# Tile 1 of layer one transposed by a DMA, other dummies at the start, and new engine lists up to K'V

## The chip, the cores and the metric

The kernel runs on one core of one Trainium2 chip. A core has five engines that run their own instruction lists and meet at semaphores: TensorE (PE; its weight loads are shown apart, as PEld), VectorE (DVE), ScalarE (ACT), GpSimd (POOL) and SyncE (SP), which issues DMAs. The metric is the device time of one execution in microseconds (us), as the median of several runs.

## What is computed

Two layers, each a linear attention and an MLP, on x of 2048 tokens by 512, in bfloat16; both layers use the same weights.

```python
def _A_ref(x, wqkv, wo):
    H = 32; Dh = D // H
    q, k, v = qkv[0], qkv[1], qkv[2]
    phi = lambda t: jnp.where(t > 0, t + 1, jnp.exp(t)) + 1e-6
    pq, pk = phi(q), phi(k)
    kv = jnp.einsum("bhsd,bhse->bhde", pk, v)
    z = jnp.einsum("bhsd->bhd", pk)
    num = jnp.einsum("bhqd,bhde->bhqe", pq, kv)
    den = jnp.einsum("bhqd,bhd->bhq", pq, z)[..., None] + 1e-6
    o = num / den
...
    h = _gelu(jnp.einsum("bsd,df->bsf", y, w1) + b1)
    return jnp.einsum("bsf,fd->bsd", h, w2) + b2
...
x = x + _A_ref(_layernorm(x, axis=-1), A_wqkv, A_wo)
x = x + _B_ref(_layernorm(x, axis=-1), B_w1, B_b1, B_w2, B_b2)
x = x + _A_ref(_layernorm(x, axis=-1), A_wqkv, A_wo)
x = x + _B_ref(_layernorm(x, axis=-1), B_w1, B_b1, B_w2, B_b2)
```

## The kernel before

The 2048 tokens are 16 tiles of 128, in four chunks of four tiles. Layer one takes the chunks in the order 3, 0, 1, 2, so tiles 12 to 15 come first, then 0 to 3 and so on. A helper records every operation with what it reads and writes, and a scheduler then issues each engine's operations strictly in the order of a list written out by hand in `CONF["ORDER"]`; waits follow from the recorded reads and writes. An engine whose next operation is not ready stands still, whatever is behind it. The scheduler's own clock decides only which buffer and which PSUM bank an operation gets.

The names in the lists carry the layer, then the tile (or chunk and part). For layer one (0), tile t:

- `statsA0_t`, `aggrA0_t` (DVE), `vepsA0_t`, `powA0_t`, `nmrA0_t` (mostly POOL), `normA0_t` (DVE or ACT): the layer norm of a tile. Tiles 12 to 15 take a variant, in which the mean is subtracted first (`cenA0_t`), and `yscA0_t` scales later; tile 13 has its statistics from ACT (`sumA0_13`, `sqA0_13`).
- The normed tile is turned so that the model dimension lies on the partitions. Either by PE, as four 128x128 transposes into a PSUM bank (`PTA0_t`, L806) and a copy out of it by ACT (`tcA0_t`, L816); or by one DMA transpose on SP's queue (`TA0_t`, L793). The table `CONF["WAY"]` says which.
- `K0_t` (L861): the keys of a tile, four matmuls of 512 columns. `Q0_c_k` (L879 and L892): the queries of chunk c. `expk`, `reluk` (ACT, L831 and L842), `mink`, `phik` (mostly DVE, L844, L848; where `WAY` says "max", L835 and L837): phi of the keys; `expq` to `phiq` the same for queries.
- `G0_t_p` (L962): instead of K'V, the kernel gathers K'y over all tiles in four PSUM banks that are held throughout, and multiplies with the weights of V once at the end (`KV0_p`, L1017). `Z0_c` (L943): the sums of the keys. `D0_c_k` (L1086): denominators, with `ln0`, `rec0` on ACT. `M0_p` (L1040): K'V with `wo` folded in. `WO0_t` (L1110): the output of the attention. `W10`, `W20` (L1142, L1181): the MLP. `RA0_t` adds the residual.
- POOL issues the late loads of the weights (L683): `wv`, `wo`, and `w1` and `w2` in two halves each. All of them, as well as `b2` and `Tb1` (the transpose of the bias b1) on SP, wait until the last DMA transpose of layer one's first norm has landed.

PE starts with dummies on constants (`warm`, `N_WARM` of 512 columns and `N_WARM2` of 128, L699), then transposes tile 12, runs eight more narrow dummies (`idle0_0`), transposes tile 13, and so on. Each of the first tiles goes the way: centred on DVE, transposed on PE, copied by ACT, read by its K.

The PE transpose of tile 1 holds one of the at most two PSUM banks that such transposes may have at a time, and its copy stands in ACT's list between `reluq0_3_3` and `yscA0_15`.

Of the kernel before, what the change touches and what calls it, by code (L numbers as in the profile page):

```python
# [282 lines left out]
def assign_waits(graph, order, sems, dma_sems):  # L283
# [56 lines left out]
    N_WARM2=4, N_IDLE=[8, 1], XQ='sp', WKQ='sp act', WK1=1,  # L340
    LAND={'x0': 3220, 'x1': 4450, 'wk1': 5200, 'wk0': 6080, 'x2': 6750, 'wq': 8250, 'xc0': 9520, 'xc1': 10800, 'xc2': 12050},
    C0=(3, 0, 1, 2), N_WARM=8, ZC=(0, 3), LQ='sp', N_HALF=1, N_K=4, N_Q=3, P_Z0=6.15, N_PB=1, N_PT=8, P_DEN=-50.43,
# [4 lines left out]
            "warm PTA0_12 idle0_0 PTA0_13 K0_12 idle0_1 K0_13 PTA0_14 Q0_3_0 Q0_3_2 PTA0_15 G0_12_0 K0_14 K0_15 "  # L347
            "Q0_3_3 Q0_3_1 G0_13_0 PTA0_1 G0_14_0 K0_0 Z0_3 G0_15_0 K0_1 K0_3 K0_2 Q0_0_2 Q0_0_3 G0_0_0 G0_1_0 Q0_0_0 "
            "K0_8 G0_2_0 G0_3_0 K0_5 Z0_0 K0_4 K0_6 K0_7 Q0_0_1 K0_10 K0_11 Q0_1_0 K0_9 Q0_1_3 Z0_1 G0_4_0 Z0_2 "
            "Q0_1_2 Q0_1_1 G0_5_0 D0_0_3 D0_0_0 G0_6_0 D0_0_1 G0_7_0 D0_0_2 G0_8_0 ZR0 G0_9_0 G0_10_0 G0_11_0 G0_11_2 "  # L350
            "D0_1_0 G0_11_1 Q0_2_0 G0_11_3 KV0_0 D0_1_1 KV0_1 D0_1_2 KV0_2 KV0_3 Q0_2_1 M0_1 M0_2 M0_0 M0_3 Q0_2_2 "
            "WO0_0_0 WO0_0_1 WO0_0_2 WO0_0_3 D0_1_3 WO0_1_0 WO0_3_0 WO0_2_0 Q0_2_3 WO0_5_0 WO0_4_0 WO0_6_0 PTB0_0 "
            "WO0_7_0 W10_0_12_0 W10_0_11_0 W10_0_13_0 W10_0_9_0 W10_0_5_0 W10_0_3_0 W10_0_4_0 W10_0_6_0 W10_0_0_0 "
            "W10_0_1_0 W10_0_8_0 W10_0_7_0 W10_0_10_0 W10_0_13_1 W10_0_4_1 W10_0_7_1 W10_0_0_1 W10_0_2_0 W10_0_11_1 "
            "WO0_8_0 W10_0_3_1 W10_0_12_1 W20_1_0 W10_0_5_1 W10_0_2_1 W20_1_7 W10_0_10_1 W10_0_6_1 W10_0_9_1 W20_0_0 "
# [25 lines left out]
            "reluq0_3_2 expq0_3_0 expk0_14 reluk0_14 normA0_3 expq0_3_2 expk0_15 reluk0_15 reluq0_3_3 tcA0_1 yscA0_15 "  # L381
            "expk0_0 expq0_3_3 reluq0_3_1 expq0_3_1 reluk0_1 expk0_1 normA0_5 normA0_8 expk0_2 reluq0_0_2 normA0_10 "
            "reluk0_3 expq0_0_3 expk0_3 normA0_6 normA0_7 expk0_8 expq0_0_0 expq0_0_2 reluq0_0_0 reluk0_5 expk0_5 "
            "expk0_4 normA0_9 reluk0_6 expk0_6 expk0_7 reluq0_0_1 expq0_0_1 expk0_10 expk0_11 reluk0_11 expk0_9 "
            "reluk0_9 expq0_1_3 expq0_1_2 expq0_1_0 reluq0_1_2 expq0_1_1 ln0_0_0 rec0_0_0 ln0_0_1 rec0_0_1 ln0_0_3 "
            "rec0_0_3 reluq0_1_1 cpz0 ln0_0_2 rec0_0_2 ln0_1_0 expq0_2_0 rec0_1_0 ln0_1_1 b1c rec0_1_1 cpm0_1 cpm0_0 "
            "cpm0_3 ln0_1_2 rec0_1_2 ln0_1_3 rec0_1_3 expq0_2_1 expq0_2_3 reluq0_2_1 reluq0_2_3 expq0_2_2 tcB0_0 "
# [91 lines left out]
            "x0 x1 wk0 x2 wq xc0 xc1 xc2 TA0_0 TA0_3 TA0_2 TA0_5 TA0_8 TA0_4 TA0_6 TA0_7 TA0_10 TA0_11 TA0_9 b1 b2 "  # L479
            "Tb1 TB0_1 TB0_2 TB0_3 TP0_2_0 TB0_5 TB0_7 TB0_6 TB0_4 TP0_3_1 TP0_3_0 TP0_3_3 TP0_2_3 TP0_2_1 TP0_2_2 "  # L480
# [7 lines left out]
        "TA0_0": "dma", "TA0_1": "pe", "TA0_10": "dma", "TA0_11": "dma", "TA0_12": "pe", "TA0_13": "pe", "TA0_14": "pe",  # L488
# [55 lines left out]
def build_kernel(nc, A_x, A_wqkv, A_wo, B_x, B_w1, B_b1, B_w2, B_b2, out, conf=None, report=False):  # L544
# [5 lines left out]
    with ExitStack() as es:  # L550
# [827 lines left out]
```

## Time and profile before

| what | value |
|---|---|
| median of 3 runs | 325.02 us (324.99 to 325.56) |
| the profiled execution's own time | 325.09 us |
| its span in the trace | 323.4 us |
| granted TensorE clock | 1.00 |
| PE busy | 319.9 us, 1725 matmuls |
| DVE, ACT, POOL busy | 215.5, 195.1, 135.4 us |

The times in the trace count from the start of the span. PE's row counts the time in which a matmul is under way; matmuls overlap, so the ends of neighbours lie over each other. A view of waits says who waited for whom; the chain of waits follows back, from the last instruction, what released each step. SPq and POOLq are the DMA queues of SP and POOL: the row of a DMA's issue is not that of its transfer.

### The profile page before, as it was taken

To read this page: it belongs to the slowest core of one execution; us is meant where nothing else is said; L and a number is where in the kernel's file an instruction comes from. 1 tells how busy PE (TensorE), PEld (TensorE's weight loads), DVE (VectorE), ACT (ScalarE), POOL (GpSimd) and SP (SyncE) were. 2 spreads that over 40 slices of the span, in tenths; PEclk is the share of its full clock that TensorE was granted. 3 is DMA by queue.
4 is the path that set the end of the run, shared out by engine and by line. 5 is a ranking of instruction groups with operands and counts; after the bars stand their busy time and mean duration, and the time that the engine had idled before them with its cause. 6 is when DMAs were issued, how large, how long until landed. Compare 5 with 4: busy or idle time off the path is not lost.

```text
span 323.4 us, 4794 instructions
## 1 busy us (share of the span) xinstructions
PE 319.9 (99%) x1725; PEld 159.1 (49%) x1725; DVE 215.5 (67%) x506; ACT 195.1 (60%) x335; POOL 135.4 (42%) x224
## 2 busy tenths in 40 slices
PE   8999999999999999999999999999999999999996
PEld 4444545675444444444444444458644444444443
DVE  5998769999985660214759999999898664000232
ACT  5999698873136129488974657879913734576000
POOL 4672278638703359000366645873902934000000
PEclk9999999999999999999999999999999999999999
DMA  7514458212320105310003200121252243000004
GB/s 246 175 39 94 146 144 305 60 34 59 72 49 12 39 16 99 67 32 2 0 0 68 49 16 2 23 59 36 50 84 49 49 53 79 16 0 2 32 25 155
DMA packets 47572, 20.52 MB, mean 63 GB/s; under 512 B 42620, under 2 KB 46076, under 8 KB 47548
## 3 DMA queue, kind: packets, MB, share of 16 engines
q1 hardware_dynamic: 46076, 15.19, 20.9%
q0 software_dynamic: 1056, 4.72, 4.6%
q10 hardware_dynamic: 416, 0.30, 0.3%
q8 instruction: 14, 0.23, 0.3%
q14 instruction: 10, 0.08, 0.1%
HBM read 8.00 MB, written 2.10 MB: 31 GB/s over the span
## 4 chain that ended last, share of the span: by engine, by line
PE 92%; DVE 6%; POOL 1%; issue 0%
PE ps L1142 30%; PE ps L1181 29%; PE ps L861 9%; PE ps L1110 7%; PE ps L962 4%; PE ps L892 3%; PE ps L879 3%; PE ps L994 2%; PE ps L699 1%; PE ps L1168 1%; DVE gtb L1007 1%; DVE rd L1065 1%; PE ps L943 1%; DVE xsb L1115 1%; DVE gacc L1004 1%; PE ps L1086 1%
## 5 line engine op out<-in xcount | busy, mean ns | idle before, releaser
L1148 ACT ACTIVATE gT<-ps,b1c 128x512 bf16<-128x512 f32 (+1 forms) x140 | 77.2, 600 | 64.4 <-PE ps L1142 63.5
L1142 PE MATMUL ps<-t,w 128*128 128x512 bf16 (+1 forms) x560 | 101.3, 337 | 0.0
L1181 PE MATMUL ps<-w,gT 128*128 128x512 bf16 x434 | 98.4, 379 | 0.0
L1142 PEld LDWEIGHTS ps<-t,w 128*128 128x128 bf16 x560 | 54.5, 98 | 43.8 <-ACT t L816 0.3
L1181 PEld LDWEIGHTS ps<-w,gT 128*128 128x128 bf16 x434 | 42.3, 98 | 50.2
L758 POOL TENSOR_TENSOR rstd<-veps,neghalf 128x1 f32<-128x1 f32 x64 | 39.3, 627 | 5.0 <-DVE veps L756 2.8
L831 ACT ACTIVATE eb<-ps 128x512 bf16<-128x512 f32 x56 | 32.4, 605 | 11.3 <-PE ps L879 3.7
L1191 DVE TENSOR_TENSOR pkb<-ps,xsb 128x512 bf16<-128x512 f32 x15 | 10.2, 685 | 41.5 <-PE ps L1181 41.5
L743 DVE BATCH_NORM_STATS2 stats<-xsb 128x6 f32<-128x512 f32 x48 | 32.1, 677 | 0.3
L861 PE MATMUL ps<-wqkv,t 128*128 128x512 bf16 x128 | 31.4, 379 | 0.0
L1110 PE MATMUL ps<-gtb,t 128*128 128x512 bf16 x128 | 31.3, 380 | 0.1
L842 ACT ACTIVATE rb<-ps 128x512 bf16<-128x512 f32 x38 | 22.8, 607 | 9.3 <-PE ps L861 7.0
L748 POOL TENSOR_SCALAR veps<-mv 128x1 f32<-128x1 f32 x32 | 9.0, 282 | 42.9 <-DVE mv L745 40.9
L756 POOL TENSOR_SCALAR veps<-mv 128x1 f32<-128x1 f32 x28 | 7.1, 258 | 45.5 <-DVE mv L745 44.1
L778 ACT ACTIVATE yb<-xsb,nmr,rstd 128x512 bf16<-128x512 f32 x21 | 16.7, 812 | 11.4 <-POOL nmr L775 11.4
L783 DVE TENSOR_SCALAR yb<-xsb,mv,rstd 128x512 bf16<-128x512 f32 x27 | 14.9, 560 | 11.9 <-POOL rstd L758 11.6
L1187 DVE TENSOR_TENSOR xsb<-ps,xsb 128x512 f32<-128x512 f32 x16 | 10.9, 682 | 16.8 <-PE ps L1181 16.8
L879 PE MATMUL ps<-wqkv,t 128*128 128x512 bf16 x80 | 20.2, 379 | 0.0
L1110 PEld LDWEIGHTS ps<-gtb,t 128*128 128x128 bf16 x128 | 12.3, 98 | 14.8 <-ACT gtb L975 0.3
L861 PEld LDWEIGHTS ps<-wqkv,t 128*128 128x128 bf16 x128 | 12.3, 98 | 14.8 <-ACT t L816 0.3
L844 DVE TENSOR_SCALAR eb<-eb 128x512 bf16<-128x512 bf16 x46 | 13.8, 312 | 8.2 <-ACT eb L831 8.0
L1127 POOL TENSOR_TENSOR xsb<-xsb,b2b 128x512 f32<-128x512 f32 x14 | 17.1, 1218 | 1.0 <-DVE yb L783 0.7
(103 smaller groups left out, 395.0 us busy)
## 6 DMA issues: line engine op xcount, KB each, us to landing
w<-in_B_w_dram POOLq DMA_DIRECT2D x4, 896.0 KB, 7.5
out_dram<-pkb SPq DMA_DIRECT2D x15, 128.0 KB, 2.0
t<-in_A_x_dram SPq DMA_DIRECT2D x3, 512.0 KB, 6.7
t<-yb SPq DMA_TRANSPOSE x57, 2.5
wqkv<-in_A_wqkv_dram SPq DMA_DIRECT2D x1, 512.0 KB, 5.2
wqkv<-in_A_wqkv_dram POOLq DMA_DIRECT2D x1, 512.0 KB, 4.3
wo<-in_A_wo_dram POOLq DMA_DIRECT2D x1, 512.0 KB, 5.7
t<-t SPq DMA_TRANSPOSE x20, 2.5
```

The costliest lines, as they stand in the source:

```text
L743: G.op("dve", lambda e: e.bn_stats(stats[:, s.slot, :], src()), 602, reads=src_keys, writes=[k + "s"], tiles=[s, *src_tiles], prio=prio, n ...
L758: G.op("pool", lambda e: e.tensor_tensor(rstd[:, s.slot:s.slot + 1], veps[:, s.slot:s.slot + 1], neghalf[:], op=ALU.pow), 530, reads=[k + ...
L778: G.op("act", lambda e: e.activation(yb[:, y.slot, :], src(), ACT.Identity, bias=nmr[:, s.slot:s.slot + 1], scale=rstd[:, s.slot:s.slot + 1]),
L831: G.op("act", lambda e: e.activation(eb[:, et.slot, :], bank(bt), ACT.Exp, scale=factor()), 569 if by else 483, reads=[src_key, *more], wr ...
L842: G.op("act", lambda e: e.activation(rb[:, rt.slot, :], bank(bt), ACT.Relu, scale=factor()), 569 if by else 478, reads=[src_key, *more], w ...
L861: ins = e.matmul(bank(b), lhsT=yTa(yT)[:, dt, k * P:(k + 1) * P], rhs=wqkv[:, dt, D:2 * D], start=(dt == 0), stop=(dt == DT - 1))
L879: ins = e.matmul(bank(b), lhsT=yTa(yT)[:, dt, k * P:(k + 1) * P], rhs=wqkv[:, dt, 0:D], start=(dt == 0), stop=(dt == DT - 1))
L1110: ins = e.matmul(bank(wb), lhsT=yTa(pq)[:, kt, k * P:(k + 1) * P], rhs=gtb[:, kt, :], start=(kt == 0), stop=(kt == DT - 1))
L1127: G.op("pool" if on_pool else "dve", lambda e: e.tensor_tensor(xsb[:, st, :], xsb[:, st, :], b2b[:], op=ALU.add), 1120 if on_pool else 600 ...
L1142: ins = e.matmul(bank(b, n), lhsT=w1[:, dt, ft * P:(ft + 1) * P], rhs=yTa(yT)[:, dt, k0 * P:k1 * P], start=(dt == 0), stop=(dt == DT - 1))
L1148: G.op("act", lambda e, ft=ft, b=b, k0=k0, k1=k1, n=n: e.activation(gT[:, g.slot, ft * 512 + k0 * P:ft * 512 + k1 * P], bank(b, n), ACT.Ge ...
L1181: ins = e.matmul(bank(b), lhsT=gT[:, g.slot, ft * 512 + k * P:ft * 512 + (k + 1) * P], rhs=w2[:, ft, :], start=(ft == 0), stop=(ft == FT - 1))
```

## The change

Tile 1 of layer one goes from PE to the DMA transpose: `PTA0_1` and `tcA0_1` are gone from the lists, `TA0_1` comes into SP's. The dummies ahead of the first transpose are seven wide and nine narrow ones instead of eight and four. And the lists of all five engines are written anew for the stretch up to K'V; behind KV0_0 the list of PE is what it was. On POOL `w1_0`, `w1_1`, `wv` and `w2_1` now follow one another directly. No function is changed.

```diff
-    N_WARM2=4, N_IDLE=[8, 1], XQ='sp', WKQ='sp act', WK1=1,
+    N_WARM2=9, N_IDLE=[8, 1], XQ='sp', WKQ='sp act', WK1=1,
...
-    C0=(3, 0, 1, 2), N_WARM=8, ZC=(0, 3), LQ='sp', N_HALF=1, N_K=4, N_Q=3, P_Z0=6.15, N_PB=1, N_PT=8, P_DEN=-50.43,
+    C0=(3, 0, 1, 2), N_WARM=7, ZC=(0, 3), LQ='sp', N_HALF=1, N_K=4, N_Q=3, P_Z0=6.15, N_PB=1, N_PT=8, P_DEN=-50.43,
...
         "pe":
-            "warm PTA0_12 idle0_0 PTA0_13 K0_12 idle0_1 K0_13 PTA0_14 Q0_3_0 Q0_3_2 PTA0_15 G0_12_0 K0_14 K0_15 "
-            "Q0_3_3 Q0_3_1 G0_13_0 PTA0_1 G0_14_0 K0_0 Z0_3 G0_15_0 K0_1 K0_3 K0_2 Q0_0_2 Q0_0_3 G0_0_0 G0_1_0 Q0_0_0 "
-            "K0_8 G0_2_0 G0_3_0 K0_5 Z0_0 K0_4 K0_6 K0_7 Q0_0_1 K0_10 K0_11 Q0_1_0 K0_9 Q0_1_3 Z0_1 G0_4_0 Z0_2 "
-            "Q0_1_2 Q0_1_1 G0_5_0 D0_0_3 D0_0_0 G0_6_0 D0_0_1 G0_7_0 D0_0_2 G0_8_0 ZR0 G0_9_0 G0_10_0 G0_11_0 G0_11_2 "
-            "D0_1_0 G0_11_1 Q0_2_0 G0_11_3 KV0_0 D0_1_1 KV0_1 D0_1_2 KV0_2 KV0_3 Q0_2_1 M0_1 M0_2 M0_0 M0_3 Q0_2_2 "
+            "warm PTA0_12 idle0_0 PTA0_13 K0_12 idle0_1 K0_13 PTA0_14 Q0_3_0 Q0_3_2 PTA0_15 G0_12_0 K0_14 Q0_3_3 "
+            "K0_15 Q0_3_1 G0_13_0 K0_0 G0_14_0 K0_1 G0_15_0 K0_2 G0_0_0 Q0_0_2 K0_3 G0_1_0 Q0_0_3 G0_2_0 K0_5 K0_8 "
+            "Z0_3 G0_3_0 Q0_0_0 K0_4 Q0_0_1 K0_6 K0_11 K0_7 Z0_0 G0_4_0 K0_10 K0_9 Z0_1 Q0_1_2 Q0_1_3 Q0_1_0 Z0_2 "
+            "G0_5_0 Q0_1_1 D0_0_0 G0_6_0 D0_0_1 G0_7_0 D0_0_2 D0_0_3 G0_8_0 D0_1_0 G0_9_0 G0_10_0 G0_11_0 G0_11_1 ZR0 "
+            "G0_11_2 Q0_2_0 G0_11_3 KV0_0 D0_1_1 KV0_1 D0_1_2 KV0_2 KV0_3 Q0_2_1 M0_1 M0_2 M0_0 M0_3 Q0_2_2 WO0_0_0 "
...
         "act":
             "wk1 sumA0_13 tcA0_12 sqA0_13 tcA0_13 expk0_12 reluk0_12 tcA0_14 expk0_13 reluq0_3_0 reluk0_13 tcA0_15 "
-            "reluq0_3_2 expq0_3_0 expk0_14 reluk0_14 normA0_3 expq0_3_2 expk0_15 reluk0_15 reluq0_3_3 tcA0_1 yscA0_15 "
-            "expk0_0 expq0_3_3 reluq0_3_1 expq0_3_1 reluk0_1 expk0_1 normA0_5 normA0_8 expk0_2 reluq0_0_2 normA0_10 "
-            "reluk0_3 expq0_0_3 expk0_3 normA0_6 normA0_7 expk0_8 expq0_0_0 expq0_0_2 reluq0_0_0 reluk0_5 expk0_5 "
-            "expk0_4 normA0_9 reluk0_6 expk0_6 expk0_7 reluq0_0_1 expq0_0_1 expk0_10 expk0_11 reluk0_11 expk0_9 "
-            "reluk0_9 expq0_1_3 expq0_1_2 expq0_1_0 reluq0_1_2 expq0_1_1 ln0_0_0 rec0_0_0 ln0_0_1 rec0_0_1 ln0_0_3 "
-            "rec0_0_3 reluq0_1_1 cpz0 ln0_0_2 rec0_0_2 ln0_1_0 expq0_2_0 rec0_1_0 ln0_1_1 b1c rec0_1_1 cpm0_1 cpm0_0 "
+            "reluq0_3_2 expq0_3_0 reluk0_14 expk0_14 expq0_3_2 expk0_15 yscA0_15 reluk0_15 normA0_3 expq0_3_1 expk0_0 "
+            "reluq0_3_1 normA0_8 reluk0_1 expk0_1 normA0_5 reluq0_3_3 expk0_2 reluq0_0_2 expq0_0_2 normA0_7 expq0_0_3 "
+            "expq0_3_3 expk0_3 reluk0_3 normA0_6 reluk0_5 expk0_5 expk0_8 normA0_10 expq0_0_0 reluq0_0_0 expk0_4 "
+            "normA0_9 expk0_6 reluk0_6 reluq0_0_1 expk0_11 expk0_7 reluk0_11 expq0_0_1 expk0_10 expk0_9 reluk0_9 "
+            "expq0_1_3 expq0_1_2 expq0_1_0 reluq0_1_2 expq0_1_1 ln0_0_0 ln0_0_1 rec0_0_0 reluq0_1_1 rec0_0_1 ln0_0_3 "
+            "rec0_0_3 ln0_0_2 rec0_0_2 cpz0 ln0_1_0 expq0_2_0 rec0_1_0 ln0_1_1 b1c rec0_1_1 cpm0_1 cpm0_0 cpm0_3 "
...
         "dve":
...
-            "mink0_13 statsA0_1 aggrA0_3 normA0_0 phik0_13 statsA0_2 aggrA0_1 aggrA0_2 mink0_14 yscA0_13 statsA0_10 "
-            "normA0_1 yscA0_14 phik0_14 normA0_2 minq0_3_0 mink0_15 statsA0_5 phik0_15 phiq0_3_0 aggrA0_5 aggrA0_10 "
-            "minq0_3_2 statsA0_8 zs0_3 phiq0_3_2 aggrA0_8 mink0_0 statsA0_6 statsA0_4 statsA0_7 aggrA0_4 aggrA0_7 "
-            "aggrA0_6 phik0_0 statsA0_9 mink0_1 minq0_3_3 aggrA0_9 mink0_2 phik0_1 phik0_2 minq0_3_1 normA0_4 "
-            "statsA0_11 minq0_0_3 mink0_3 phiq0_3_3 phiq0_0_3 phik0_3 aggrA0_11 phiq0_3_1 mink0_8 phik0_8 minq0_0_0 "
+            "mink0_13 statsA0_1 aggrA0_3 aggrA0_1 normA0_0 statsA0_2 phik0_13 aggrA0_2 normA0_1 yscA0_13 mink0_14 "
+            "phik0_14 normA0_2 yscA0_14 statsA0_8 mink0_15 aggrA0_8 phik0_15 statsA0_7 statsA0_5 minq0_3_1 mink0_0 "
+            "minq0_3_0 aggrA0_5 phik0_0 statsA0_11 phiq0_3_1 statsA0_6 aggrA0_7 mink0_1 phiq0_3_0 phik0_1 minq0_3_2 "
+            "aggrA0_11 aggrA0_6 statsA0_4 mink0_2 aggrA0_4 phik0_2 phiq0_3_2 statsA0_9 statsA0_10 normA0_4 aggrA0_10 "
+            "mink0_3 minq0_0_3 phik0_3 aggrA0_9 phiq0_0_3 normA0_11 minq0_3_3 minq0_0_2 zs0_3 mink0_5 mink0_8 "
...
         "pool":
             "id0 bdm0 neghalf id1 bdm1 powA0_12 vepsA0_13 eps6 powA0_13 powA0_14 vepsA0_0 powA0_15 b1z powA0_0 "
-            "vepsA0_3 powA0_3 nmrA0_3 vepsA0_1 powA0_1 vepsA0_2 powA0_2 vepsA0_5 powA0_5 nmrA0_5 vepsA0_8 powA0_8 "
-            "vepsA0_10 powA0_10 nmrA0_10 nmrA0_8 vepsA0_7 vepsA0_4 powA0_7 powA0_4 vepsA0_9 vepsA0_6 powA0_6 powA0_9 "
-            "nmrA0_7 nmrA0_6 vepsA0_11 powA0_11 nmrA0_9 phik0_6 w1_1 phiq0_1_2 wv wo w2_1 phiq0_1_1 w1_0 pr0_0_2 "
+            "vepsA0_1 powA0_1 vepsA0_2 powA0_2 vepsA0_3 powA0_3 nmrA0_3 vepsA0_8 powA0_8 nmrA0_8 vepsA0_5 powA0_5 "
+            "nmrA0_5 vepsA0_7 vepsA0_6 powA0_7 nmrA0_7 vepsA0_4 powA0_4 vepsA0_11 powA0_6 nmrA0_6 vepsA0_10 powA0_11 "
+            "powA0_10 vepsA0_9 powA0_9 nmrA0_9 nmrA0_10 phik0_6 w1_0 w1_1 wv w2_1 phiq0_1_2 phiq0_1_1 wo pr0_0_2 "
...
         "sp":
-            "x0 x1 wk0 x2 wq xc0 xc1 xc2 TA0_0 TA0_3 TA0_2 TA0_5 TA0_8 TA0_4 TA0_6 TA0_7 TA0_10 TA0_11 TA0_9 b1 b2 "
-            "Tb1 TB0_1 TB0_2 TB0_3 TP0_2_0 TB0_5 TB0_7 TB0_6 TB0_4 TP0_3_1 TP0_3_0 TP0_3_3 TP0_2_3 TP0_2_1 TP0_2_2 "
+            "x0 x1 wk0 x2 wq xc0 xc1 xc2 TA0_0 TA0_1 TA0_2 TA0_3 TA0_8 TA0_5 TA0_7 TA0_4 TA0_6 TA0_11 TA0_10 TA0_9 b1 "
+            "Tb1 b2 TB0_1 TB0_2 TB0_3 TP0_2_0 TB0_5 TB0_7 TB0_6 TB0_4 TP0_3_1 TP0_3_0 TP0_3_3 TP0_2_3 TP0_2_1 TP0_2_2 "
...
     WAY={
-        "TA0_0": "dma", "TA0_1": "pe", "TA0_10": "dma", "TA0_11": "dma", "TA0_12": "pe", "TA0_13": "pe", "TA0_14": "pe",
+        "TA0_0": "dma", "TA0_1": "dma", "TA0_10": "dma", "TA0_11": "dma", "TA0_12": "pe", "TA0_13": "pe", "TA0_14": "pe",
```

## The prediction, made before the result was known

> **What bounds the kernel now.** I read the page first: the span and the engines.
>
> ```profile
> span 323.4 us, 4794 instructions
> PE 319.9 (99%) x1725; PEld 159.1 (49%) x1725; DVE 215.5 (67%) x506; ACT 195.1 (60%) x335; POOL 135.4 (42%) x224
> ```
>
> TensorE is busy in 319.9 of 323.4 us, but a busy PE row may hide short waits, because ends of matmuls are modelled. So the view of waits comes next, for PE alone, and it has a single line, the start of the kernel:
>
> ```profile
> PE ps L699 <- PEq L1363: 0.8, 1, 0.8
> ```
>
> Next the busy time by stretch (columns: window, its length, then PE, PEld, DVE, ACT, POOL with counts, clock, share of DMA, GB/s), for the stretch that the change reorders:
>
> ```profile
> 10.00:22.00 12.00, 12.00 (x77) 5.83 (x76) 11.96 (x40) 12.00 (x22) 8.28 (x23) 1.00 0.25 66
> 22.00:34.00 12.00, 12.00 (x71) 5.63 (x70) 9.40 (x31) 11.51 (x22) 4.38 (x12) 1.00 0.43 88
> 46.00:58.00 12.00, 12.00 (x69) 5.88 (x68) 10.90 (x23) 10.05 (x20) 9.59 (x12) 1.00 0.88 290
> ```
>
> PE is full in all of it; from 10 to 22 us DVE (11.96 of 12) and ACT (12.00 of 12) are full as well. The chain of waits gives the same picture step by step (start, length, what):
>
> ```profile
> 0.83 4.00 PE ps L699 x12
> 4.83 0.43 PE ps L806 x4
> 5.26 0.72 PE ps L699 x8
> 5.98 0.22 PE ps L806 x4
> 6.20 0.86 PE ps L861 x4
> ...
> 15.52 0.22 PE ps L806 x4
> ...
> 51.07 0.86 PE ps L1040 x4
> ```
>
> The first five groups begin each where the last ends, and so it goes on through the stretch. Four 128-wide transposes take 0.43 us at 4.83 and 0.22 us at 5.98: the array runs at half speed until about 5.7 us, and at full speed after. The reader is to see that the end of this kernel is the sum of what PE issues: the change can move it only by what it takes from or adds to PE's list, or by a wait that PE does not have today.
>
> **The change, part by part.**
>
> *The transpose taken off PE.* PTA0_1 is the group of four at 15.52: it goes, minus 0.22 us. Nothing hides behind it, since PE is gapless there, so the whole of it counts. Its copy out of PSUM, tcA0_1, goes from ACT as well (first row below): 0.69 us of relief for an ACT that is full, worth nothing to the end directly, because PE is no faster for it, but slack for the new lists.
>
> ```profile
> 16.37 0.69 ACT L816 ACTIVATE t<-ps 128x512 bf16<-128x512 bf16 x1
> 12.15 1.30 SPq L793 DMA_TRANSPOSE t<-yb  x1
> SPq L793 <- ACT eb L831: 11.9, 5, 6.0
> t<-yb SPq DMA_TRANSPOSE x57, 2.5
> ```
>
> *The transpose put on SP's queue.* One more DMA transpose: 1.30 us of issue, 2.5 us to landing. The queue of SP waits 11.9 us in five waits before such transposes (third row, the queue's own waits; the longest 6.0), so there is room for 1.3 us more. Who needs it, and when? In the new list K0_0 stands directly behind G0_13_0, where the transpose stands today: at 15.52, or 15.63 with the dummies' 0.11 (below). Then G0_14_0 and K0_1, 0.86 us each step (a group of four, as in the row at 6.20): K0_1 at 17.35. TA0_0 starts at 12.15 as today and lands at 12.15 + 2.5 = 14.65, one us ahead of K0_0. TA0_1 needs normA0_1, today the DVE step at 14.24:
>
> ```profile
> 14.24 0.41 DVE L783 TENSOR_SCALAR yb<-t,mv,rstd 128x512 bf16<-128x512 bf16 x1
> ```
>
> In the new list a min, a scaling and a statistic no longer stand ahead of it, so it can be done behind TA0_0's issue, at 13.5, and TA0_1 lands at 16.0. Even where it is today, done at 14.65, the transposed tile is there at 17.15, still before 17.35. So both cost nothing; without that cover the price is the lateness itself, one for one, paid by K0_1 and all behind it. The transposes behind, up to TA0_9, are shifted into the queue's waits.
>
> *The dummies.* One wide less, five narrow more. The weight loads show the half-speed steps: 0.15 busy after 0.28 idle, so 0.43 us, for a wide one, and 0.86 us for eight narrow, 0.107 each.
>
> ```profile
> 3.34 0.15 PEld L699 LDWEIGHTS ps<-const-bfloat16-1.0 128*128 128x128 bf16 x1 [0.28 <-issue]
> 4.94 0.86 PEld L699 LDWEIGHTS ps<-const-bfloat16-1.0 128*128 128x128 bf16 x8
> 5.29 0.60 ACT L816 ACTIVATE t<-ps 128x512 bf16<-128x512 bf16 x1 [0.49 <-PE ps L806]
> 5.79 0.71 ACT L738 ACTIVATE eb<-t,stats 128x512 bf16<-128x512 bf16 x1
> 6.49 0.59 ACT L816 ACTIVATE t<-ps 128x512 bf16<-128x512 bf16 x1
> 7.13 0.55 PEld L861 LDWEIGHTS ps<-wqkv,t 128*128 128x128 bf16 x4 [0.34 <-ACT t L816]
> ```
>
> Five times 0.107 less 0.43 is +0.11 us before the first transpose. Does it reach the end? The last row says K0_13's weight load waited for ACT. That ACT chain has no air: tcA0_12 starts at 5.29, where the first transposes end (4.83 + 0.43), then sqA0_13, then tcA0_13, back to back, to 7.08. All of it starts 0.11 later, so K0_13 does, and from there PE is full. Bounds: 0 if ACT could catch up, 0.11 if not; the rows show no gap, so I take +0.11.
>
> *K, Q, G, Z and D reordered on PE, with evictions, norms and adds on ACT, DVE and POOL.* The work is the same, so PE's sum is unchanged; the question is only whether some operand is late. The largest jump forward is G0_0_0: two steps (G0_15_0, K0_2) behind K0_1's end, so at about 19.9. It needs phik0_0, which DVE ends at 21.48 today:
>
> ```profile
> 17.51 0.64 ACT L831 ACTIVATE eb<-ps 128x512 bf16<-128x512 f32 x1
> 18.76 1.87 DVE L743 BATCH_NORM_STATS2 stats<-t 128x6 f32<-128x512 bf16 x3
> 20.82 0.66 DVE L837 SCALAR_TENSOR_TENSOR pkb<-ps,eb 128x512 bf16<-128x512 f32 x1
> 23.73 0.68 ACT L842 ACTIVATE rb<-ps 128x512 bf16<-128x512 f32 x1
> ```
>
> Three statistics (1.87 us by the second row), four aggregates, one min and two adds that stand ahead of it today come behind it, one min comes ahead: over 2 us of room. What sets it then is its exponent expk0_0 (first row: 17.51 to 18.15), which the new ACT list does not put later; with a min between, phik0_0 ends by about 19.1, and G0_0_0 has 0.8 us. The other way goes reluk0_3 (last row): two exponents of Q, one of K and normA0_7 come ahead of it, some 0.6 to 0.8 us each, while tcA0_1 and normA0_10 no longer do, so it is about 1.2 us later, 24.9 to 25.6, and G0_3_0 keeps its time on PE: the tightest place I find. I take 0 for the reordering, as every row of PE's list is covered so far as I can follow it, and 0.3 us as the upper bound of the forecast's own case.
>
> *POOL's weight loads.* Now w1_0, w1_1, wv and w2_1 go out one behind the other, and wo comes behind them and behind phiq0_1_1.
>
> ```profile
> 35.20 0.94 POOL L683 DMA_DIRECT2D w<-in_B_w_dram  x1
> 42.98 0.79 POOL L683 DMA_DIRECT2D wqkv<-in_A_wqkv_dram  x1
> 47.52 0.74 POOL L683 DMA_DIRECT2D w<-in_B_w_dram  x1
> w<-in_B_w_dram POOLq DMA_DIRECT2D x4, 896.0 KB, 7.5
> wqkv<-in_A_wqkv_dram POOLq DMA_DIRECT2D x1, 512.0 KB, 4.3
> wo<-in_A_wo_dram POOLq DMA_DIRECT2D x1, 512.0 KB, 5.7
> 43.97 0.63 ACT L1090 ACTIVATE lr<-lr 128x512 f32<-128x512 f32 x1
> 45.74 0.58 ACT L842 ACTIVATE rb<-ps 128x512 bf16<-128x512 f32 x1
> 46.40 1.17 POOL L848 TENSOR_TENSOR t<-eb,rb 128x512 bf16<-128x512 bf16 x1 [0.88 <-ACT rb L842]
> ```
>
> The group at 51.07 above is M0, which reads wo. When does wo land? phiq0_1_1 waits for reluq0_1_1 on ACT, which moves ahead of three logarithm and exponent steps, from 45.74 to 43.97; so phiq0_1_1 goes from 46.40 to about 44.6, ends at 45.8, and wo is issued there. If it lands 4.3 us later, as wv does with nothing queued ahead, that is 50.1; with 5.7, as wo does behind wv, 51.5. M0 needs it at 51.07 - 0.11 = 50.96. Is the queue clear by then? Today wv, wo, w2_1 and w1_0 (2.88 MB) went from 42.98 to about 55.0 (47.52 + 7.5): 0.24 MB/us with the gaps, and 0.29 by the window from 46 to 58. The new queue up to wo's end holds 3.81 MB, from 35.20 on (w1_0 now stands where w1_1 stood): 13.1 to 15.9 us, so 48.3 to 51.1. I take 50.1, with nothing in front, since the four ahead have ten us of their own before it: no wait. Upper bound 51.5: 0.5 us. wv itself is safe: 2.36 MB end by 45.0 at the slower rate, and its first reader comes near 48.9. Tb1 and b2 swap on SP; b2 is read first in the MLP, and the copy of the turned bias stands in ACT's list where it stood: nothing.
>
> *Sum.* Profile's own time 325.09 (span 323.4, and 1.7 around it), minus 0.22, plus 0.11, plus 0: 324.98. The median of the runs is 0.07 below that execution, so 324.91. The forecast's own range runs from no charge for the dummies (324.8) to the reordering's 0.3 on top (325.2). What this kernel's measurement can tell from no change is about 0.2%, 0.65 us; the sum is a sixth of that.
>
> **The rivals.**
>
> *wo late.* M0's four matmuls take over as a wait, since wo now stands behind 3.3 MB. For it: from 46 to 58 the share of DMA is 0.88 today. Against: the queue should be clear. Price 0.5 - 0.11: 325.4; it passes 0.65 us only if wo lands after 51.7.
>
> *Slower: ACT becomes the bound between 22 and 28 us.* Place: reluk0_3 and phik0_3, then G0_3_0, and through the held PSUM banks the next K. It decides once ACT runs about 0.7 us behind the list, which is full (12.00 of 12, then 11.51 of 12), so it cannot recover before 34. Price: two steps, 0.68 + 0.6, about 1.3: 326.2. Against it: ACT has lost 0.69 us of work and DVE none gained.
>
> *The clock rises later.* Half speed ends near 5.7 us, 4.9 after the first dummy. If the new mix of dummies made it rise as late again, at 10.6, PE would do 4.4 us of real work at half speed, about 2.2 us lost: 327.0. Against: PE is as continuously busy as before, and no row ties the rise to width. The Trainium skill (TensorE: Matmul & The Clock Gate, Part 1) says the gate is opened by a free-running window of about 3.4 us of activity, and that the instant differs by about half a us between runs; by that, a window missed would be an estimated 1.7 us and 326.6, and a shift of the instant would touch both kernels alike. The trace agrees with a rise after more than one such window, and shows one execution only.
>
> *Faster by more.* It would need 0.65 us; PE has the 0.22, and a gap before K0_13 that is under 0.34 by the weight load's row. With both and no charge for the dummies 324.5. That the transposition buys nothing at all, because the dummies give 0.11 of it back, is the forecast itself.
>
> **How the numbers follow.** Forecast 0.65; wo late 0.15, of which a third beyond 0.65 us; ACT the bound 0.12, nearly all beyond; the clock 0.03; faster by a gap closed 0.05, mostly still within 0.2%. Slower by over 0.2%: 0.05 + 0.11 + 0.03 = 0.19; faster 0.03; the same 0.78. Predicted 324.9. The range reaches down to 324.5 and up to 326.0, to hold wo late and part of the ACT case.
>
> **What would show it.** Right: sixteen transposes (four tiles) on PE in the first 20 us instead of twenty; K0_13 about 0.11 later; no new line in PE's waits; DMA transposes twelve in the first 33 us; M0 at about 50.9. Wrong: PE idle before L1040 with wo as releaser (first rival), or PE idle between 22 and 34 us behind ACT or DVE; the second four transposes at 0.43 us instead of 0.22 mean the clock. A time over 325.7 or under 324.4 refutes the sum.

## The result, and the profile after

The changed kernel takes 326.22 us (median of 10 runs, 325.44 to 326.83) against 325.24 us of the kernel before on the same chip (10 runs): ratio 1.0024, interval 1.0014 to 1.0034. It is slower by 0.24%, about 0.8 us by the ratio and 1.0 by the medians; the forecast was 324.9, and 326.22 lies over the range's upper end of 326.0. The profiled execution took 326.21 us. Its page begins:

```profile
span 324.5 us, 4796 instructions
PE 319.8 (99%) x1725; PEld 158.7 (49%) x1725; DVE 216.9 (67%) x506; ACT 194.7 (60%) x334; POOL 137.5 (42%) x224
```

PE is busy for as long as before (319.8 to 319.9), so the 1.1 us that the span grew are not work but waits. The view of PE's waits, which had one line, has three:

```profile
PE ps L699 <- PEq L1363: 0.8, 1, 0.8
PE ps L892 <- DMA t<-yb: 0.8, 1, 0.8
PE ps L861 <- DVE pkb L837: 0.3, 1, 0.3
```

L892 waits for a DMA transpose, L861 for DVE. The chain of waits of this kernel (start, length, what) shows where both are:

```profile
17.00 4.35 DMA t<-yb
21.34 0.05 issue
21.39 1.04 PE ps L892 x4
22.43 0.86 PE ps L861 x4
...
30.83 0.18 ACT eb L831
31.01 0.30 issue
31.31 0.58 ACT rb L842
31.90 0.50 ACT eb L831
32.39 0.02 issue
32.42 0.30 DVE eb L835
32.72 0.02 issue
32.74 0.70 DVE pkb L837
33.45 0.04 issue
33.49 1.04 PE ps L861 x4
```

The first is Q0_0_2, the first reader of tile 3's turned tile: TA0_3 went out at 17.00 and landed 4.35 us later, not 2.5. Without a wait Q0_0_2 would have begun at 20.40 (its predecessor's start, 19.54, and 0.86); it began at 21.39: a gap of 0.99. The second is K0_7, which waits for a PSUM bank that phik0_4 (DVE, L837) frees: 33.49 instead of 33.02, 0.47. Note that a wait costs more than the waits view says. In PE's timeline a matmul of 512 columns starts 0.22 us after the one before and its modelled end lies 0.38 after its start, and idle time counts from that end: the 0.83 and 0.30 of idle, each with 0.16 more, are the 0.99 and 0.47. (In the chain such a group stands with 1.04 instead of 0.86.)

The account closes. K0_13 begins at 6.91 instead of 7.13 (below), the transpose saves its 0.22, and two gaps cost 1.46: 1.46 - 0.22 - 0.22 = 1.02 of the 1.1 us of span. All of it lies ahead of M0, which begins at 52.02 instead of 50.91; from there to the end both kernels take 272.45 us (272.44 to 272.55 in all 14 profiles of this document), so nothing behind M0 has a part in it. Busy time by stretch (window, length, PE, PEld, DVE, ACT, POOL with counts, clock, DMA share, GB/s):

```profile
10.00:22.00 12.00, 11.17 (x55) 4.81 (x52) 11.47 (x39) 11.42 (x20) 8.43 (x18) 1.00 0.36 87
22.00:34.00 12.00, 11.70 (x69) 5.37 (x68) 9.53 (x30) 10.26 (x20) 6.30 (x16) 1.00 0.33 66
```

The 0.83 and 0.30 that PE lacks in these two rows are the two waits. ACT is less full than before in both of these stretches (11.42 and 10.26 instead of 12.00 and 11.51), DVE in the first (11.47 instead of 11.96; in the second 9.53 instead of 9.40). Neither is full; each waits in its turn.

Two views show what stood beside the two late operands. In the view of DMA queues for 18.8 to 20.4 us (packets, MB, share of 16 engines) two fetches of instructions, of 16 and 8 KB, lie inside TA0_3's flight:

```profile
q8 instruction: 1, 0.02, 5.5%
...
q14 instruction: 1, 0.01, 1.2%
```

And POOL's small steps are longer. First the kernel after (veps, L756; the power to rstd, L758; nmr, L775), then DVE beside them, then POOL in the kernel before:

```profile
13.32 0.71 POOL L756 TENSOR_SCALAR veps<-mv 128x1 f32<-128x1 f32 x1 [0.38 <-DVE mv L745]
14.11 0.77 POOL L758 TENSOR_TENSOR rstd<-veps,neghalf 128x1 f32<-128x1 f32 x1
...
28.22 0.94 POOL L758 TENSOR_TENSOR rstd<-veps,neghalf 128x1 f32<-128x1 f32 x1
29.26 0.81 POOL L775 TENSOR_SCALAR nmr<-mv,rstd 128x1 f32<-128x1 f32 x2
```

```profile
13.14 0.38 DVE L783 TENSOR_SCALAR yb<-t,mv,rstd 128x512 bf16<-128x512 bf16 x1
13.44 0.35 DVE L768 TENSOR_SCALAR yb<-yb,rstd 128x512 bf16<-128x512 bf16 x1
13.70 0.28 DVE L844 TENSOR_SCALAR eb<-eb 128x512 bf16<-128x512 bf16 x1
14.02 0.42 DVE L848 TENSOR_TENSOR pkb<-eb,rb 128x512 bf16<-128x512 bf16 x1
```

```profile
14.18 0.22 POOL L756 TENSOR_SCALAR veps<-mv 128x1 f32<-128x1 f32 x1
14.48 0.59 POOL L758 TENSOR_TENSOR rstd<-veps,neghalf 128x1 f32<-128x1 f32 x1
```

vepsA0_2 takes 0.71 instead of 0.22, and powA0_2 0.77 instead of 0.59, beside an unbroken row of short bf16 steps on DVE; later powA0_9 takes 0.94, and nmrA0_9 and nmrA0_10 behind it 0.81 together. By the Trainium skill (SBUF — State Buffer, "SBUF: two separate sides"), DVE and GpSimd share a pair of SBUF ports as an exclusive lock, held for the whole instruction by a DVE step in a 2-port mode, or by one with two SBUF inputs against a GpSimd step that reads SBUF, and the loser stands still. These rows agree with it, though they show neither the mode nor the lock.

### The profile page after: what moved, and what is told of

It reads as the page before. It is cut to its first block, busy times and chain, and to the rows that moved or that the text cites. A ratio compares the mean times of both kernels' runs of the same rounds, so it can differ in the third digit from the quotient of the medians.

```text
span 324.5 us, 4796 instructions
## 1 busy us (share of the span) xinstructions
PE 319.8 (99%) x1725; PEld 158.7 (49%) x1725; DVE 216.9 (67%) x506; ACT 194.7 (60%) x334; POOL 137.5 (42%) x224
## 4 chain that ended last, share of the span: by engine, by line
PE 85%; DVE 8%; DMA 3%; POOL 1%; SPq 1%; issue 1%; ACT 0%; ACTq 0%
PE ps L1142 30%; PE ps L1181 29%; PE ps L1110 7%; PE ps L861 6%; PE ps L892 3%; PE ps L962 3%; PE ps L994 2%; PE ps L879 2%; DMA t<-in_A_x_dram 2%; DVE stats L743 1%; DMA t<-yb 1%; PE ps L1168 1%; DVE gtb L1007 1%; DVE rd L1065 1%; POOL rstd L758 1%; PE ps L943 1%
## 5 line engine op out<-in xcount | busy, mean ns | idle before, releaser
L758 POOL TENSOR_TENSOR rstd<-veps,neghalf 128x1 f32<-128x1 f32 x64 | 39.7, 631 | 5.1 <-DVE veps L756 3.0
L831 ACT ACTIVATE eb<-ps 128x512 bf16<-128x512 f32 x56 | 32.3, 600 | 11.8 <-PE ps L879 3.7
L861 PE MATMUL ps<-wqkv,t 128*128 128x512 bf16 x128 | 31.9, 379 | 0.4 <-DVE pkb L837 0.3
L756 POOL TENSOR_SCALAR veps<-mv 128x1 f32<-128x1 f32 x28 | 8.4, 304 | 45.0 <-DVE mv L745 43.6
L748 POOL TENSOR_SCALAR veps<-mv 128x1 f32<-128x1 f32 x32 | 9.1, 284 | 42.8 <-DVE mv L745 40.8
L778 ACT ACTIVATE yb<-xsb,nmr,rstd 128x512 bf16<-128x512 f32 x21 | 16.7, 812 | 11.4 <-POOL nmr L775 11.4
L879 PE MATMUL ps<-wqkv,t 128*128 128x512 bf16 x80 | 20.4, 379 | 0.0
L861 PEld LDWEIGHTS ps<-wqkv,t 128*128 128x128 bf16 x128 | 12.1, 98 | 16.0 <-DVE pkb L837 0.8
```

Of the source, the lines that this page charges most:

```text
L758: G.op("pool", lambda e: e.tensor_tensor(rstd[:, s.slot:s.slot + 1], veps[:, s.slot:s.slot + 1], neghalf[:], op=ALU.pow), 530, reads=[k + ...
L778: G.op("act", lambda e: e.activation(yb[:, y.slot, :], src(), ACT.Identity, bias=nmr[:, s.slot:s.slot + 1], scale=rstd[:, s.slot:s.slot + 1]),
L831: G.op("act", lambda e: e.activation(eb[:, et.slot, :], bank(bt), ACT.Exp, scale=factor()), 569 if by else 483, reads=[src_key, *more], wr ...
L861: ins = e.matmul(bank(b), lhsT=yTa(yT)[:, dt, k * P:(k + 1) * P], rhs=wqkv[:, dt, D:2 * D], start=(dt == 0), stop=(dt == DT - 1))
L879: ins = e.matmul(bank(b), lhsT=yTa(yT)[:, dt, k * P:(k + 1) * P], rhs=wqkv[:, dt, 0:D], start=(dt == 0), stop=(dt == DT - 1))
```

## The experiments

Theory A1: tile 3 now stands fourth on SP's queue, its transpose has 1 us to spare where it had 2.7, and a fetch inside its flight (theory F) uses that up. Theory A2: K0_7's wait comes through POOL and ACT, from the stretched powA0_9 (theory P: POOL's steps are longer beside certain rows of DVE steps) and from nmrA0_10 standing behind it. All runs, each against the kernel before on the same chip:

| kernel | us | before | ratio (95%) |
|---|---|---|---|
| dummies_only | 325.47 | 325.32 | 1.0002 (0.9993 to 1.0011) |
| after_old_dummies | 326.29 | 325.32 | 1.0025 (1.0014 to 1.0037) |
| lists_only | 326.15 | 325.32 | 1.0026 (1.0016 to 1.0036) |
| fetch_later | 326.60 | 325.32 | 1.0037 (1.0025 to 1.0049) |
| nmr10_first | 326.15 | 325.57 | 1.0014 (1.0002 to 1.0026) |
| tile3_early | 325.94 | 325.57 | 1.0013 (1.0004 to 1.0022) |
| both_early | 325.54 | 325.57 | 1.0004 (0.9993 to 1.0015) |
| before_6_13 | 325.55 | 325.57 | 0.9998 (0.9989 to 1.0007) |
| after_again | 326.42 | 325.48 | 1.0037 (1.0022 to 1.0051) |
| dve_order | 326.05 | 325.48 | 1.0021 (1.0013 to 1.0030) |
| dve_order_nmr10 | 325.64 | 325.48 | 1.0005 (0.9997 to 1.0014) |
| tile1_only | 325.79 | 325.48 | 1.0021 (1.0005 to 1.0037) |

**The change taken apart.** dummies_only puts the new dummies into the kernel before; after_old_dummies puts the old ones into the kernel after.

```diff
-    N_WARM2=4, ...  N_WARM=8
+    N_WARM2=9, ...  N_WARM=7
```

> The kernel before with seven wide and nine narrow dummies, nothing else changed. Theory A (a transposed tile, tile 3's, comes late because an instruction fetch of 16 KB runs on the DMA engines while it is in flight: 4.35 us to landing instead of 2.4 to 2.5): the eight added PE instructions bring the fetch from 19.8 to about 19.0 us, where no transpose of this kernel is in flight (one lands at 18.0, the next is issued at 21.6), so nothing comes late; K0_13 starts up to 0.11 later: 325.2 to 325.4. Rival B (the dummies or the clock cost the time by themselves): 326.2.

> The kernel after with eight wide and four narrow dummies as before. Theory A: eight PE instructions fewer ahead of it, the fetch comes about 0.8 us later, at 19.6 to 19.7, when tile 3's transposed tile (issued at 17.0) has all but landed: 2.4 to 2.5 us to landing, no wait of Q0_0_2 (0.99 gone), the second wait of 0.47 behind it smaller or gone: 324.6 to 325.1. Rival B (dummies or clock): the same time, but then the kernel before with the new dummies is slow too. Rival C (tile 3's late place in the lists, without the fetch): 4.3 us to landing again and 326.1. Rival D (the longer SP queue by the tile's move): 326.1 as well.

The dummies cost nothing that can be seen, in either kernel: rival B falls. (325.47 lies just over the 325.2 to 325.4 that were expected; beside the kernel before's 325.32 the ratio is 1.0002.) The second forecast failed: 326.29 instead of 324.6 to 325.1. In its profile the fetch still met TA0_3, only later (at 19.33; landing 3.26 us after issue, 20.32, in time for Q0_0_2), so in this one execution there was no first gap, but K0_7's gap of 0.47 was there all the same. So the second wait does not follow from the first. A new one of 0.31 stood at Q0_0_3, which waited for ACT (eb, L831). This execution had a span of 323.9 us, and its 326.29 lies 2.4 above it; in the other six runs the time is 1.7 to 1.8 above spans of 323.8 to 325.2. So this profile does not show what held the longer of them.

lists_only keeps tile 1 on PE within the new lists:

```diff
-... G0_13_0 K0_0 G0_14_0 ...        (PE)
+... G0_13_0 K0_0 PTA0_1 G0_14_0 ...
-... reluk0_15 normA0_3 expq0_3_1 ... (ACT)
+... reluk0_15 normA0_3 tcA0_1 expq0_3_1 ...
-        "TA0_1": "dma"
+        "TA0_1": "pe"
```

> The new lists alone: eight wide and four narrow dummies, tile 1 turned by TensorE (its four matmuls behind K0_0, the copy behind normA0_3 on ACT, no DMA transpose of it). By 17 us PE has run as many instructions as in the kernel after (eight fewer dummy ones, eight more of the transposes). Theory A: the fetch comes at 18.9 again, tile 3's transpose is in flight from 17.0, lands 1 to 2 us late, Q0_0_2 waits up to 1 us: 325.8 to 326.5. Rival D (the tile's move to the DMA queue costs the time): no late landing, 325.2 to 325.4. Rival C (the lists without the fetch): 326.2.

As A1 said: 326.15, and TA0_3 takes 4.11 us to landing. The gaps in its profile are 0.18 at Q0_0_2, 0.46 at K0_7, and 0.31 at K0_1, which waits for the copy of tile 1 and is this kernel's own. So the late landing and both waits are there without the DMA transpose of tile 1, and rival D is not needed for them. That the time comes out as high as the kernel after's rests in part on the 0.31 that only this kernel has: the two waits are 0.64 here.

tile1_only is the other half, the transpose in the old lists:

```diff
-... G0_13_0 PTA0_1 G0_14_0 ...   (PE)
+... G0_13_0 G0_14_0 ...
-x0 ... TA0_0 TA0_3 TA0_2 ...     (SP)
+x0 ... TA0_0 TA0_1 TA0_3 TA0_2 ...
+            hold = [Tile(psum, "hold", "t0")] if tag == "A0_1" else []
```

> Tile 1 turned by the DMA alone: the kernel before with its lists and dummies, without PTA0_1 and tcA0_1, its DMA transpose second in SP's queue (a PSUM bank stays taken by it, so that the banks of all later steps are as before). Tile 3's transpose now stands third, issued at about 16.2 instead of 14.3, with its first reader K0_3 at 19.4. Theory A1 (it is the place of tile 3 behind tile 1 that is exposed): landing at 18.7 without a fetch, at 20 to 20.5 with one in it; Z0_3 may wait 0.3 for the held bank; 325.3 without the fetch, 325.8 to 326.4 with it. Rival L (the move costs nothing, only the new lists do): 325.1 to 325.4.

Between the two: 325.79, 1.0021, with an interval down to 1.0005; three of its twelve runs took 327.06 to 327.80, and no profile shows why. Its profile has Z0_3's 0.30 for the held bank, an artefact of the experiment, and TA0_3 at 16.38 with 3.55 us to landing, in time for K0_3 at 20.50. Alone, the transposition also moves tile 3 back by 2.1 us, but what it costs without the held bank stays open.

**Where the fetch falls.** fetch_later and before_6_13 were to move the fetch by the number of PE instructions ahead of it.

```diff
-... idle(f"idle{n}_{k}", [P] * cf["N_IDLE"][k], ...      N_IDLE=[8, 1]   (fetch_later)
+... idle(f"idle{n}_{k}", ([P] if k else [D]) * ...       N_IDLE=[2, 1]
-    N_WARM2=4, ... N_WARM=8                               (before_6_13)
+    N_WARM2=13, ... N_WARM=6
```

> The kernel after, with only the filler dummies behind the first transposes changed: two of 512 columns in place of eight of 128, the same columns, twelve PE instructions fewer. Theory A: the fetch comes about 1.2 us later, at about 20.1, behind tile 3's landing; it may hit tile 8's transpose instead (issued at 19.3, its reader is at 25), which has time: no wait of Q0_0_2, 324.8 to 325.3. Rivals B, C and D: nothing that they name has changed, 326.2.

> The kernel before with six wide and thirteen narrow dummies. Theory F (the fetch of instructions delays a transpose in flight): eight more PE instructions than in the run with seven and nine, whose fetch came at 18.16, 0.01 us ahead of tile 2's landing: the fetch now comes at 16.5 to 17.5, inside tile 2's transpose (15.7 to 18.2), which lands 3 to 4.4 us after its issue instead of 2.41; K0_2 needs it at 20.3, so the time stays at 325.3 to 325.6. Rival (the late landings of tile 3 have to do with the new lists or with the transposes around it, not with a fetch): 2.4 to 2.5 us wherever the fetch lies.

In both the 16 KB fetch did not move as expected: it came at 19.04 and at 19.96, in the first inside TA0_3's flight again (4.27 us to landing, a gap of 0.91, and 326.60 instead of 324.8 to 325.3), in the second in no transpose's (the time, 325.55, was as expected under either view, so it decides nothing). What sets its instant stays open. In all 14 profiles the first fetch of this stretch, of 8 or of 16 KB, begins between 17.80 and 19.33: the kernel before has no transpose in flight from 18.01 to 21.58, the kernel after has TA0_3 in flight from 17.00. And after_again, the unchanged kernel after, moved it by itself:

> The kernel after, unchanged, for a second profile and for a comparison on the same chip. Theories A1 and A2: K0_7's gap of 0.47 is there to 0.01 us again, since POOL's powA0_9 takes 0.94 again; Q0_0_2's gap is anything from 0 to 1.0, by whether a fetch falls into tile 3's transpose: 326.0 to 326.5.

In its profile the fetch came at 17.82, inside tile 2's transpose. The chain there:

```profile
16.00 3.97 DMA t<-yb
19.97 0.14 issue
20.11 0.59 PE ps L861 x2
```

Now TA0_2 takes 3.97 us and K0_2 (L861) has the gap, 0.75, while Q0_0_2 has none; K0_7's is 0.47 again. (At the start this execution also waited 0.9 us for a load of weights and 0.3 for tile 12's input.) Same kernel, same lists: what is late is the transpose that meets the fetch. Over all 14 profiles (counted from the records of the DMA queues) layer one has 164 transposes of this kind. 137 landed within 2.56 us of their issue; 27 took 2.66 to 4.35. In 26 of these 27 an instruction fetch was running later than 1.1 us after the issue, and the last stood behind a late one; of the 137 that holds for four, and there the fetch began within 0.25 us of the landing. The 1.1 us were found from these rows; they are not a rule. Later in the kernel, with other transfers about, the tie is looser: of 644 such transposes 94 took over 2.6 us, 86 of these with such a fetch, and 36 with one did not. So fetch and late landing are tied by their instants; that the fetch is the cause was not tested, as no run could place a fetch at will. In the kernel before it was there too, at 31.74 to 34.81, on a tile that PE did not wait for (DMA view of that window):

```profile
q14 instruction: 1, 0.01, 0.6%
...
t<-yb SPq DMA_TRANSPOSE x1, 3.1
```

The Trainium skill (Runtime: NRT & Kernel Launch, "Instruction fetch mechanics") says that an engine refills its instructions in blocks of 16 KiB through a DMA queue of its own, at a cost mostly hidden. The 16 KB packets agree, the 8 KB ones are not in it; here the cost does not stay hidden, if it falls on a neighbour's transfer as these rows suggest.

**The two waits taken away.** nmr10_first moves one step of POOL:

```diff
-... powA0_10 vepsA0_9 powA0_9 nmrA0_9 nmrA0_10 ...
+... powA0_10 nmrA0_10 vepsA0_9 powA0_9 nmrA0_9 ...
```

> The kernel after with one POOL step moved: nmrA0_10 right behind powA0_10, no longer behind nmrA0_9. Theory A2 (K0_7's wait comes through POOL and ACT: powA0_9 takes 0.94 us instead of 0.55, nmrA0_10 stands behind it though its own operand is ready at 26.9, and normA0_10 at the head of ACT's list holds three steps behind it): normA0_10 starts about 0.7 earlier, K0_7's gap of 0.47 is gone, Q0_0_2's wait is as in the kernel after: 326.2 - 0.47, so 325.6 to 325.9. Rival (the second wait is an echo of the first, or phik0_4 is late by something else): the gap stays, 326.2.

The gap at K0_7 is gone. POOL and ACT (normA0_10, L778, which ACT had waited for until 30.11 in the kernel after) and PE's waits in this kernel:

```profile
27.59 0.27 POOL L775 TENSOR_SCALAR nmr<-mv,rstd 128x1 f32<-128x1 f32 x1
28.31 0.22 POOL L756 TENSOR_SCALAR veps<-mv 128x1 f32<-128x1 f32 x1 [0.46 <-DVE mv L745]
28.62 0.95 POOL L758 TENSOR_TENSOR rstd<-veps,neghalf 128x1 f32<-128x1 f32 x1
...
29.61 0.86 ACT L778 ACTIVATE yb<-t,nmr,rstd 128x512 bf16<-128x512 bf16 x1
```

```profile
PE ps L699 <- PEq L1363: 0.8, 1, 0.8
PE ps L892 <- DMA t<-yb: 0.7, 1, 0.7
PE ps L806 <- DVE yb L724: 0.7, 1, 0.7
```

powA0_9 still takes 0.95, but nothing that matters stands behind it. The third line is tile 13's centred input, late at the start of this execution. The time, 326.15, missed the expected 325.6 to 325.9, but the kernel before took 325.57 on this chip. The ratio falls from 1.0024 and 1.0037 to 1.0014, with intervals that overlap: here the trace, and not the time, shows that the wait is gone.

tile3_early removes the first wait, by giving TA0_3 data that is there early:

```diff
-                return e.dma_start_transpose(dst, yb[:, y.slot, :])
+                return e.dma_start_transpose(dst, yb[:, src.slot, :])
+            src, ykey = from0 or (y, ykey)
-... TA0_0 TA0_1 TA0_2 TA0_3 ...
+... TA0_0 TA0_1 TA0_3 TA0_2 ...
```

> The kernel after with tile 3's DMA transpose reading tile 0's normalized tile, which is there at 12.2 us, and issued ahead of tile 2's: it leaves out the use of tile 3's own data in K and Q, all else runs as in the kernel after. Theory A1 (tile 3's turned tile is what Q0_0_2 waits for, in most executions and by up to 0.99): it lands at about 17.3, tile 2's at about 18.6 just ahead of K0_2 at 18.7; no gap at Q0_0_2; the gap of 0.47 at K0_7 stays: 325.4 to 325.8, and the runs lie closer together than the 1.4 us between the kernel after's. Rival (the first wait is a chance of the one profiled execution): 326.2.

> Both edits, nmrA0_10 right behind powA0_10 and tile 3's transpose from tile 0's data: leaves out the use of tile 3's own data in K and Q. Theories A1 and A2 together: no gap on PE but the short one at K0_13; what is left is the sum of the prediction, 324.9 to 325.3. If something else of the change costs time as well, a rest over 325.5 shows it.

tile3_early has no gap at Q0_0_2 and K0_7's 0.47 unchanged (third line of its waits; the first is tile 12's input, late in this execution):

```profile
PE ps L807 <- DVE veps L756: 1.0, 1, 1.0
PE ps L699 <- PEq L1366: 0.8, 1, 0.8
PE ps L862 <- DVE pkb L838: 0.3, 1, 0.3
```

Its ratio is 1.0013 (325.94, over the expected 325.4 to 325.8), and its runs lie within 0.85 us of each other (the kernel after's within 1.4). With both edits the view of PE's waits is:

```profile
PE ps L699 <- PEq L1366: 0.8, 1, 0.8
PE ps L807 <- DVE yb L724: 0.2, 1, 0.2
```

and the kernel takes as long as the one before (1.0004). By the times alone, up to 0.15% could be left, the upper end of the interval; and the expected 324.9 to 325.3 was missed with 325.54: the kernel before took 325.57 on this chip, and the 0.22 of the transpose does not show.

The starts on PE close the account. From tile 14's transposes (PTA0_14) to M0 it takes 42.90 us in the kernel before, so 42.68 without the transpose of tile 1. The kernel after takes 44.23, that is 42.68, the two gaps of 0.99 and 0.47, and 0.09. nmr10_first takes 43.55, which is 42.68 and its one gap of 0.87; tile3_early 43.15, which is 42.68 and 0.47; both edits 43.02. The last 0.34 are two delays too short for the view of waits: 0.17 at K0_2 (19.32), whose transpose this edit puts behind tile 3's (it lands at 19.18), and 0.16 at Q0_0_3, again behind ACT's exponent (L832), as in after_old_dummies. So the two waits are what the change lost, and with them gone two short ones used up the transpose's 0.22 in this profile.

**Two repairs that use all data.** dve_order changes seven steps on DVE, so that a statistic runs beside vepsA0_2; dve_order_nmr10 has nmr10_first's edit as well.

```diff
-aggrA0_2 normA0_1 yscA0_13 mink0_14 phik0_14 normA0_2 yscA0_14 statsA0_8
+aggrA0_2 normA0_1 yscA0_13 statsA0_8 normA0_2 mink0_14 phik0_14 yscA0_14
```

> The kernel after with the order of seven DVE steps changed: statsA0_8 and normA0_2 come ahead of mink0_14 and phik0_14. Theory P (POOL's vepsA0_2 takes 0.71 us instead of 0.22 and powA0_2 0.77 instead of 0.58 because DVE runs a row of short bf16 steps beside them): with a statistic beside them they take about 0.3 and 0.58, so tile 3's normalization and its transpose come about 0.5 earlier (issued at 16.4 to 16.5 instead of 17.0) and Q0_0_2's gap is at most 0.5; K0_7's gap stays 0.47: 325.6 to 326.0. Rival (vepsA0_2 is slow for POOL's own reasons, by its place behind powA0_1): 0.71 again and the time of the kernel after.

> Both repairs with all data used: the order of DVE as in the run before this one, and nmrA0_10 right behind powA0_10 on POOL. Theories A1, A2 and P: no gap at K0_7, at most 0.5 at Q0_0_2: 325.1 to 325.6, as fast as the kernel before or up to 0.2 faster. If it stays at 325.9 or more, the repairs give their gain back elsewhere.

POOL in dve_order:

```profile
13.46 0.51 POOL L756 TENSOR_SCALAR veps<-mv 128x1 f32<-128x1 f32 x1 [0.38 <-DVE mv L745]
14.05 0.57 POOL L758 TENSOR_TENSOR rstd<-veps,neghalf 128x1 f32<-128x1 f32 x1
```

Beside the statistic powA0_2 has its 0.57 again; vepsA0_2, which still meets normA0_1 and yscA0_13, falls only to 0.51, less than expected. TA0_3 goes out 4.37 us after TA0_0 instead of 4.76; it met the fetch again (4.27 us to landing), and the gap was 0.42. The time, 326.05, is just over what was expected. So these two steps do depend on what DVE runs beside them; for powA0_9 no run was made to change that, and there it is argued only. Both repairs bring 325.64, ratio 1.0005: level with the kernel before, no better. K0_7's gap is gone, but 0.58 of gap, more than the 0.5 expected at most, is still at Q0_0_2 in its profile.

## Why the prediction was wrong

*Right.* PTA0_1's 0.22 left PE, and PE's busy time was not what changed. TA0_1, forecast to land at 16.0, landed at 16.06. G0_0_0 began at 19.54 with phik0_0 done at 19.30 (forecast 19.9 and 19.1), no wait. reluk0_3, the tightest place found, came at 26.60; less the gap of 0.99 ahead of it 25.6, the upper end of what was forecast, and G0_3_0 did not wait.

*wo.* Its issue in the timeline of the kernel after, its landing in the DMA view (KB, us from issue to landing), and its reader M0 in PE's timeline:

```profile
46.88 0.78 POOL L683 DMA_DIRECT2D wo<-in_A_wo_dram  x1
```

```profile
wo<-in_A_wo_dram POOLq DMA_DIRECT2D x1, 512.0 KB, 4.4
```

```profile
52.02 1.03 PE L1040 MATMUL ps<-wo,kvb 128*128 128x512 bf16 x4
```

46.88 less the shift of 1.1 is the 45.8 forecast, 4.4 us the 4.3 taken; it landed at 51.3, 0.7 ahead of M0. That rival did not happen.

*The dummies' 0.11* was not to be seen. Tile 12's transposes (the first row of PE's timeline here; 0.63 in the kernel before) ran at full speed already, and K0_13 (the second row) came 0.22 earlier, not 0.11 later:

```profile
4.64 0.40 PE L806 MATMUL ps<-idp,yb 128*128 128x128 bf16 x4
...
6.91 1.04 PE L861 MATMUL ps<-wqkv,t 128*128 128x512 bf16 x4
```

The way was the one forecast, through ACT's copies (tcA0_12 began at 5.07 instead of 5.29); what differed was the instant at which the matmuls went from half to full speed: the last step of 0.107 us between two narrow ones begins at 4.30 here and at 5.58 in the kernel before. It is not the new mix that did this: in lists_only and after_old_dummies, with the old dummies, that step begins at 4.52 and 4.73, and tile 13's transposes at 5.51 and 5.41, against 5.82 in the kernel before. The instant varies from one execution to the next.

*The step that failed* is the landing of the transposes: "One more DMA transpose: 1.30 us of issue, 2.5 us to landing", and "The transposes behind, up to TA0_9, are shifted into the queue's waits." For the transposes behind TA0_1 that was argued from the queue's room and never from their readers. TA0_3 moved from second place, issued at 14.28 for a reader at 19.46, to fourth place, issued at 17.00 for a reader at 20.40. Its margin shrank from 2.7 us to 1.0, and 2.5 was a median over 57 rows: single transposes of the kernel before took 3.1 (at 31.74) and, later on, up to 4.5. A landing 0.8 to 1.9 us late, priced at nothing, came to a gap of 0.99 in the profiled execution, and in after_again to 0.75 at K0_2. That a late landing costs this is shown, by tile3_early; why it is late, the fetch, is tied by instants only.

*The second failed term* is "I take 0 for the reordering", with 0.3 as its bound. It was mis-sized: 0.47. The prediction followed two operands, phik0_0 and reluk0_3, and not the path through POOL. The change moved nmrA0_10 from its place right behind powA0_10 to behind nmrA0_9, so that powA0_9's 0.94 (0.55 in the kernel before) went through nmrA0_9, nmrA0_10, ACT's list and phik0_4 to K0_7.

*The rival of ACT as the bound* gave 326.2, which is the time, but by luck and not by its way: reluk0_3 and G0_3_0 held, and ACT stood idle (0.75 us ahead of normA0_10). A list that waits in order is not an engine that is full.

*Slips in the working* that change nothing: the queue up to wo's end holds 3.80 MB, not 3.81; 324.9 and 2.2 for the clock are 327.1, not 327.0; and the starts of PTA0_1 and M0, 15.52 and 51.07, are those of chain rows, which begin where the row before ends, while the first matmuls start at 15.36 and 50.91.

## What to carry to other kernels

When a list is reordered, work out for each moved transfer the margin from its landing to its first reader, with the slowest landing in the trace and not the median; a transfer that is early enough hides a chance delay, one with 1 us to spare pays it often (a gap behind a late transpose stood in seven of the eight profiles that had the new lists and used all data). Durations of small steps on POOL belong to what DVE runs beside them, so do not carry them over into a new order. And where an engine's list is strict, a step whose operand is ready should not stand behind one that is still waiting.

## What the runs showed of the hardware

Of 164 DMA transposes of layer one's first norm, 137 landed 2.40 to 2.56 us after issue; 27 took 2.66 to 4.35, and 26 of these had a fetch of instructions in their flight (the 4.35 one of 16 KB and one of 8 KB). The two go together in time; that one causes the other was not tested. POOL's stretching repeats: vepsA0_2 took 0.712 us in all five profiles with its neighbourhood unchanged, and powA0_9 0.939 to 0.942, while the instant of the fetch differed by 1.5 us between them.
